# Four small copies inside the chip's memory are issued after the last weight transfer instead of ahead of three

## The chip, the core and the metric

The kernel runs on one core of one Trainium2 chip. A core has a matrix engine (TensorE, "PE" in the profile, with "PEld" for its weight loads), a vector engine (VectorE, "DVE"), a scalar engine (ScalarE, "ACT"), a general engine (GpSimd, "POOL") and a synchronisation engine (SyncE, "SP"). Each has its own instruction stream. Data comes into the on-chip memory (SBUF) and leaves it by 16 DMA engines; POOL, SP and ACT issue such transfers on queues of their own. Matrix products land in PSUM, which has eight banks.

The metric is device time in microseconds (us) of the one core. Lower is better.

## What is computed

Two stages in a row. The first is linear attention with a learned feature map, for 8 batches, 8 heads, 576 rows and 64 channels:

```python
def phi(x):
    proj = einsum('bhsd,df->bhsf', x, w_phi)
    proj = proj - max(abs(proj), axis=-1)
    return concatenate([exp(proj), exp(-proj)], axis=-1)
kv  = einsum('bhsf,bhsd->bhfd', phi(k), v);  z = sum(phi(k), axis=2)
x   = einsum('bhsf,bhfd->bhsd', phi(q), kv) / (einsum('bhsf,bhf->bhs', phi(q), z) + 1e-6)
```

The heads are then laid side by side, so that x is 8 x 576 x 512. The second stage mixes channels in the frequency domain, with one complex 512 x 512 matrix for each of the 64 lowest frequencies:

```python
X = rfft(x, axis=1);  Y = zeros_like(X)
Y[:, :64] = einsum('bmd,mde->bme', X[:, :64], w_r + 1j * w_i)
u = x + irfft(Y, n=576, axis=1)
out = u + relu(u @ w_ch)
```

The weights w_r and w_i are 64 x 512 x 512 each in float32; they are nearly all of the kernel's input.

## The kernel before, in words

**Attention.** Sixteen units (four groups of two heads by four pairs of batches) are worked through in a software pipeline. Their result stays in SBUF as xs, in bf16, and the forward transform of each group is a product with a table of cosines and sines.

**Weights.** The 64 frequencies are handled as eight "octets" o = 0 to 7 of eight frequencies, for each of the four groups g of 128 input channels, and for the real (i = 0) and imaginary (i = 1) matrix. That makes 64 weight tiles of 1 MB in bf16. `wload` (line 341) issues each as one transfer on POOL's queue, which converts from float32 on the way. `next_w` (line 362) takes the next key from the list wq and issues it. A tile pool of nine buffers (tag "wt") holds the tiles. In the last stage four of the buffers are taken by other tiles, so five weights fit. The last 16 keys, those of octets 6 and 7, are the late ones (`LATE`, line 356). A weight is used by `mix` (line 474): eight matmuls into one PSUM tile.

**Last stage.** The loop at line 941 takes the remaining mixes one by one. After each mix it asks for one more weight, with four exceptions (line 954), and then hands out a share of other work: `fill` (line 829) pops steps of a hand-written list with costs in microseconds. The list holds products of x with w_ch (`Channels`, 696), steps that turn finished octets for the inverse transform (`relay`, 795), and steps that add the inverse transform of octets 0 to 5 to all rows (`Absorb`, 736). In `keep_w` (760) half of the Absorb steps have ACT copy a bank to a tile rl, and POOL add it to the tile xw; the rest have ACT write xw itself.

When the last mix of an octet is done, its result y (8 frequencies, real and imaginary, 8 batches: 128 rows of 512) is copied from PSUM to a tile yst. For octets 6 and 7, z = y @ w_ch is also computed and copied to zst. The tiles yst and zst have two buffers each. The "late rows" tile yl holds y and z of octets 6 and 7 turned so that frequency lies on partitions and batch inside: `put` (line 837) moves a 128 x 512 tile to 16 partitions of yl by a transfer from SBUF to SBUF, and each tile goes to two places. For octet 6 POOL issues these four transfers, for octet 7 SP does:

```python
def put(src, o, copies):
    for s in copies:
        r = 32 * s + 16 * (o - 6)
        (pool if o == 6 else sp).dma_start(yl[r:r + 16], src)
```

**Last rows.** The `Last` objects (line 843) finish the output. For each pair of rows `base` brings the two sums (x plus what was absorbed, and its product with w_ch) into PSUM; `late` (876) adds the inverse transform of octets 6 and 7 by matmuls that read yl; the first rows read yst and zst directly instead (`straight`). Then come the relu, the sum and the store, which SP issues. Some of the `base` steps stand ahead of the last mix.

Every engine executes its instructions in the order in which the program makes them (lines are reported as that of a helper, L38, so that groups are told by their tiles). A transfer that POOL or SP issues stands in that engine's stream like any other instruction: what it has to wait for, everything behind it waits for too. Transfers on POOL's queue are taken up in the order of their issue. Eight semaphores are used in turn for them, and a transfer waits until the one that used its semaphore before has landed.

Of the kernel before, what the change touches and what calls it, by code (L numbers as in the profile page):

```python
# [44 lines left out]
def kernel(  # L45
# [295 lines left out]
    def wload(g, w):  # L341
        wt = home(g, w)
        o, i = w // 2, w % 2
        w = (moe_w_r, moe_w_i)[i]
        pool.dma_start(
            wt.rearrange("p m r e -> p m (r e)"),
            w[MG * o:MG * o + MG, g * 128:(g + 1) * 128, :].rearrange(
                "m (p r) e -> p m (r e)", r=2))
        return wt
# [3 lines left out]
    wq = [(g, mg) for g in range(NG) for mg in range(during[g])]  # L353
# [8 lines left out]
    def next_w(n):  # L362
        for _ in range(n):
            if wq:
                key = wq.pop(0)
                wts[key] = wload(*key)
# [107 lines left out]
    def mix(g, w, wt, XT, bank):  # L474

        o, i = w // 2, w % 2
        together = range({6: 2, 7: 0}.get(o, g), NG) if 2 * o >= during[g] else (g,)
        first, last = i == 0 and g == together[0], i == 1 and g == together[-1]
        XT = kept[:, g] if o == 7 and g < 2 else XT[..., 4 * o:4 * o + 4]
        if first:  # L480
            pys[o] = bank()
        py = pys[o]
        for r in range(2):
            for j in range(4):
                pe.matmul(
                    py[32 * j:32 * j + 32, :],
                    lhsT=XT[:, i, r, :, :, :, j].rearrange("p t x b -> p (t x b)"),
                    rhs=wt[:, j, r, :], start=(first and r == 0), stop=(last and r == 1),
                )
        if last and g == 0:  # L490
            act.copy(yacc[:, o, :], pys.pop(o))
        elif last and g < NG - 1:
            dve.tensor_tensor(
                out=yacc[:, o, :], in0=pys.pop(o), in1=yacc[:, o, :], op=ALU.add)
# [103 lines left out]
    def bank(shape=(128, DMODEL), dt=F32):  # L598
        return pst.tile(list(shape), dt, name="pt", tag="pt")
# [195 lines left out]
    def relay(b):  # L795

        assert turned >= (7 if b < 2 else 6)
        at = slice(0, 6 + (b < 2))
        n = 16 * at.stop
        cols = [yTa[:, dc, b, at].rearrange("p o k -> p (o k)") for dc in range(4)]  # L800
        py, pz = two_banks()
        py = py.bitcast(BF16)[:, 0:512]
        for dc in range(4):
            pe.transpose(py[:n, 128 * dc:128 * dc + 128], cols[dc], ident_b)
        for dc in range(4):
            pe.matmul(pz[:n], lhsT=cols[dc], rhs=wchb[:, dc, :],
                      start=(dc == 0), stop=(dc == 3))
        dve.tensor_copy(yall[:n, b], py[:n])
        act.copy(zall[:n, b], pz[:n])
# [14 lines left out]
    for at, b in ((24, 1), (22, 0), (17, 3), (14, 2), (7, 5), (5, 4)):  # L824
        tail.insert(at, (1.25, lambda b=b: relay(b)))
    todo[-2:] = [(1.25, lambda: relay(6)), todo[-2], (1.25, lambda: relay(7)), todo[-1]] + tail
    owed, turned = 0.0, 0

    def fill(n):
        nonlocal owed  # L830
        owed += n
        while todo and owed > 0:
            cost, f = todo.pop(0)
            owed -= cost
# [6 lines that stand above are left out]
# [100 lines left out]
    while mixq:  # L941
        key = mixq.pop(0)
        g, o, i = key[0], key[1] // 2, key[1] % 2
        if key not in wts:
            next_w(1)
        if not mixq:
            assert not todo
            for c in seq[:2]:
                c.base(1)
            for c in (seq[0], seq[2]):  # L950
                c.base(0)
        mix(*key, wts.pop(key), XTb[g % 2], bank)
        left = len(mixq)
        if left not in (LATE + 11, LATE + 1, LATE, LATE - 3):
            next_w(1)
        n = 3.4 if left > 1 else 99.0 if left else 0.0
        if g == NG - 1 and i == 1:
            end = left == 0
            py = pys.pop(o)
            yst = pb.tile([128, DMODEL], BF16, name="yst")  # L960
            pt = [bank([128, 2, 128], BF16) for h in range(2)]
            yT = [pb.tile([128, 2, 128], BF16, name=f"yT{h}") if o > 5 else None
                  for h in range(2)]
            for h in range(2):
                at = slice(H * h, H * h + H)
                if not end:
                    dve.tensor_tensor(out=yst[:, at], in0=py[:, at], in1=yacc[:, o, at],
                                      op=ALU.add)
                elif h:
                    act.copy(yst[:, at], py[:, at])  # L970
                else:
                    dve.tensor_copy(yst[:, at], py[:, at])
            if o > 5:
                put(yst, o, (0, 2))
            if not end:
                fill(0.8 if o != 5 else 0.0)
            for h in range(2):
                for dc in range(2):
                    pe.transpose(pt[h][:, dc, :],
                                 yst[:, H * h + 128 * dc:H * h + 128 * dc + 128], ident_b)  # L980
                src = pt[h].rearrange("p c (k b) -> p c b k", b=B_)
                into = yTa[:, 2 * h:2 * h + 2, :, o] if o < 6 else None
                if h != end:
                    dve.tensor_copy(*((into, src) if o < 6 else (yT[h], pt[h])))
                else:
                    act.copy(*((into, src) if o < 6 else (yT[h], pt[h])))
            turned = o + 1
            if o < 6:
                fill(n - 1.1)
                continue  # L990
            if o == 6:
                for h in range(2):
                    dve.tensor_copy(
                        yTa[:, 2 * h:2 * h + 2, 0:2, 6],
                        yT[h].rearrange("p c (k b) -> p c b k", b=B_)[:, :, 0:2])
            if end:
                seq[0].straight(0)
                seq[0].keep_p()
                seq[2].straight(0, (0,))
            else:  # L1000
                fill(0.8)
            cut = (slice(0, 384), slice(384, DMODEL))
            pz = [bank([128, e.stop - e.start]) for e in cut]
            for e in range(2):
                for h in range(2):
                    for dc in range(2):
                        pe.matmul(
                            pz[e], lhsT=yT[h][:, dc, :], rhs=wchb[:, 2 * h + dc, cut[e]],
                            start=(h == dc == 0), stop=(h == dc == 1))
            zst = pb.tile([128, DMODEL], BF16, name="zst")  # L1010
            act.copy(zst[:, cut[0]], pz[0])
            dve.tensor_copy(zst[:, cut[1]], pz[1])
            put(zst, o, (1, 3))
            fill(n - 2.4 if left else 0)
        else:
            fill(n)
# [70 lines left out]
```

## Time and profile before

| what | value |
|---|---|
| median of 3 runs | 437.31 us (435.58 to 438.34) |
| the profiled execution's own time | 435.97 us |
| its span, first to last instruction | 434.2 us |
| busy: PE / DVE / ACT / POOL | 77% / 69% / 65% / 26% of the span |
| mean granted clock of PE | 0.905 |
| POOL's queue (q0) | 85.27 MB, 100.8% of 16 engines' span |
| weight transfers: size, median time from issue to landing | 1024 KB, 25.4 us (w_r), 25.7 us (w_i) |
| the copies to yl that POOL issues: size, median to landing | 128 KB; 20.9 us (y), 19.5 us (z) |
| the copies to yl that SP issues | 128 KB; 3.6 us (y), 3.8 us (z) |
| stores of pairs of rows | 16 of 512 KB, 3.2 us to landing |

Times inside the execution are microseconds from the start of the span. "Busy" is the time in which an engine had an instruction in work. The granted clock is the share of full speed that the chip let PE run at. A chain of waits is followed back from the last instruction: at each step to what released it, or to the instruction before it on its engine. In the timeline an instruction's wait stands in brackets with what ended it. The name yl<-yst x2 means two transfers that read yst and write yl.

### The profile page before, as it was taken

What the parts mean: (1) busy time and instruction counts of PE and PEld (TensorE: products, weight loads), DVE (VectorE), ACT (ScalarE), POOL (GpSimd) and SP (SyncE); (2) the same over time, 40 slices, a digit from 0 to 9 for tenths busy, and PEclk for the clock granted to TensorE, in tenths of its full rate; (3) what the DMA queues carried; (4) which work ended last, traced back from release to release, by engine and by line L of the source; (5) the groups of instructions that cost most, each with busy time, mean ns of one, the idle gap of its engine ahead of it and who ended that gap; (6) DMA issues with size and microseconds to landing.
All of it is one profiled execution on the core that took longest, in us unless ns stands there. A gap on an engine that the chain in (4) does not pass through costs nothing.

```text
span 434.2 us, 10105 instructions
## 1 busy us (share of the span) xinstructions
PE 336.4 (77%) x4208; PEld 202.1 (47%) x4252; DVE 298.6 (69%) x585; ACT 283.2 (65%) x483; POOL 114.4 (26%) x154
## 2 busy tenths in 40 slices
PE   2577778688688578786787787957899999968994
PEld 1345556555465455554554555633344444423321
DVE  5668686765886866977977878696634447643685
ACT  3787696786986966877876877435344456643782
POOL 6232132123221412322221210210121047530073
PEclk9979697789998976989998988988899999997998
DMA  9999999999999999999999999999999999996788
GB/s 214 209 212 209 238 212 237 232 218 239 237 211 239 213 234 264 211 239 212 235 227 216 246 226 210 211 212 212 212 212 212 212 211 212 217 201 114 242 346 332
DMA packets 49821, 97.71 MB, mean 225 GB/s; under 512 B 2288, under 2 KB 11632, under 8 KB 49776
## 3 DMA queue, kind: packets, MB, share of 16 engines
q0 software_dynamic: 45088, 85.27, 100.8%
q1 hardware_dynamic: 4528, 11.73, 7.4%
q8 instruction: 33, 0.54, 0.4%
q10 hardware_dynamic: 160, 0.07, 0.1%
q14 instruction: 12, 0.10, 0.1%
HBM read 163.64 MB, written 9.44 MB: 399 GB/s over the span
## 4 chain that ended last, share of the span: by engine, by line
PE 42%; DVE 22%; ACT 16%; DMA 12%; issue 6%; POOL 0%; POOLq 0%; ACTq 0%; DVEq 0%
PE pt L38 15%; PE one L38 15%; PE two L38 8%; ACT AB L38 7%; DMA wt<-in_moe_w_i_dram 5%; DVE mk L38 5%; DVE m L38 5%; DMA kb<-in_k_dram 5%; PE pp L38 4%; ACT AQ L38 3%; ACT XT L38 2%; DVE xs L38 2%; DMA qb<-in_q_dram 2%; DVE XT L38 2%; DVE yacc L38 1%
## 5 line engine op out<-in xcount | busy, mean ns | idle before, releaser
L38 ACT ACTIVATE AB<-two 128x1024 bf16<-128x1024 f32 x64 | 62.0, 1024 | 11.0 <-DVE mk L38 8.3
L38 ACT ACTIVATE AQ<-two 128x1024 bf16<-128x1024 f32 x64 | 62.6, 1045 | 2.1 <-PE two L38 2.0
L38 DVE TENSOR_REDUCE m<-two 128x8 f32<-128x1024 f32 x32 | 39.2, 1224 | 17.2 <-PE two L38 17.1
L38 ACT CAST xw<-pt 128x512 bf16<-128x512 f32 x45 | 26.4, 586 | 36.6 <-PE pt L38 36.6
L38 PE MATMUL pt<-wchb,xT 128*128 128x512 bf16 x135 | 38.9, 400 | 9.3 <-DVE xT L38 7.3
L38 POOL DMA_DIRECT2D wt<-in_moe_w_r_dram x30 | 22.4, 747 | 87.6 <-PE pt L38 39.9
L38 DVE TENSOR_REDUCE mk<-two 128x8 f32<-128x1024 f32 x32 | 38.9, 1217 | 7.7 <-PE two L38 7.7
L38 DVE TENSOR_TENSOR va<-vn,ee 128x1152 bf16<-128x1152 f32 x32 | 42.2, 1361 | 0.0
L38 PE MATMUL two<-w2blk,qT 128*128 128x256 bf16 x128 | 23.5, 315 | 21.4 <-ACT AB L38 9.8
L38 POOL DMA_DIRECT2D wt<-in_moe_w_i_dram x28 | 21.0, 750 | 65.4 <-PE one L38 36.8
L38 PEld LDWEIGHTS <-xs 128*128 128x128 bf16 x624 | 31.5, 102 | 12.5 <-issue 6.0
L38 ACT COPY qT<-one 128x512 bf16<-128x512 bf16 (+1 forms) x32 | 19.4, 641 | 25.6 <-PE one L38 25.2
L38 PEld LDWEIGHTS <-qT 128*128 128x128 bf16 x144 | 15.1, 107 | 36.0 <-issue 31.7
L38 PE MATMUL two<-mT,minus 96*128 96x512 bf16 x64 | 27.0, 423 | 3.1 <-issue 1.1
L38 PEld LDWEIGHTS <-AQ 128*128 128x128 bf16 x512 | 24.2, 107 | 7.9 <-issue 4.3
L38 DVE TENSOR_TENSOR xs<-one,rd 128x384 bf16<-128x384 f32 x48 | 26.7, 557 | 1.6
L38 PE MATMUL two<-w2blk,kT 128*128 128x256 bf16 x128 | 20.6, 288 | 9.2 <-ACT AB L38 9.2
L38 PE MATMUL one<-kvz,AQ 128*128 128x65 bf16 x512 | 26.9, 207 | 1.0 <-ACT qT L38 0.8
L38 DVE COPY xT<-pt 128x512 bf16<-128x512 bf16 x36 | 16.8, 470 | 14.9 <-PE pt L38 14.9
L38 DVE RECIPROCAL rd<-one 128x6 f32<-128x6 f32 x48 | 9.4, 195 | 25.2 <-PE one L38 25.2
L38 PE MATMUL one<-wt,XT 128*32 128x512 bf16 x272 | 24.7, 452 | 1.7 <-DMA kb<-in_k_dram 1.7
L38 PEld LDWEIGHTS <-xT 128*128 128x128 bf16 x168 | 15.3, 103 | 21.9 <-DVE xT L38 8.0
(163 smaller groups left out, 735.8 us busy)
## 6 DMA issues: line engine op xcount, KB each, us to landing
wt<-in_moe_w_r_dram POOLq DMA_DIRECT2D x30, 1024.0 KB, 25.4
wt<-in_moe_w_i_dram POOLq DMA_DIRECT2D x28, 1024.0 KB, 25.7
out_dram<-of SPq DMA_DIRECT2D x16, 512.0 KB, 3.2
vn<-in_v_dram POOLq DMA_DIRECT2D x13, 576.0 KB, 23.6
kb<-in_k_dram POOLq DMA_DIRECT2D x16, 288.0 KB, 19.2
qb<-in_q_dram POOLq DMA_DIRECT2D x16, 288.0 KB, 17.0
xs<-in_moe_w_i_dram POOLq DMA_DIRECT2D x2, 1024.0 KB, 23.8
vn<-in_v_dram SPq DMA_DIRECT2D x3, 576.0 KB, 5.3
```

What stands on the lines that cost most here:

```text
L38: ins = f(*args, **kwargs)
```

## The change

The tile pair of octet 6 is kept in a variable `staged` instead of being copied at once. In the loop, after each possible issue of a weight, the four copies are issued if the list of weights is empty and the pair has not been copied yet. For octet 7 (`end` is true) the copies stay where they were, on SP.

```diff
-    owed, turned = 0.0, 0
+    owed, turned, staged = 0.0, 0, None
...
         left = len(mixq)
         if left not in (LATE + 11, LATE + 1, LATE, LATE - 3):
             next_w(1)
+        if not wq and staged:
+            put(staged[0], 6, (0, 2))
+            put(staged[1], 6, (1, 3))
+            staged = None
         n = 3.4 if left > 1 else 99.0 if left else 0.0
...
-            if o > 5:
+            if end:
                 put(yst, o, (0, 2))
             if not end:
                 fill(0.8 if o != 5 else 0.0)
...
             dve.tensor_copy(zst[:, cut[1]], pz[1])
-            put(zst, o, (1, 3))
+            if end:
+                put(zst, o, (1, 3))
+            else:
+                staged = yst, zst
             fill(n - 2.4 if left else 0)
```

In the changed program the order of instructions is the same on PE, DVE, ACT and SP. On POOL the four copies move from between the fourth- and third-last weight transfers to just after the last one. Three weight transfers and five of POOL's additions (xw<-rl,xw) that stood behind the first copies, or between them, now stand ahead of them.

## The prediction

> **What bounds the kernel now.** I read the page's slices and queues first, then the chain of work that ended last, then POOL's and PE's order of time around the change, and last the clock by windows.
>
> From the page: busy share of the DMA engines and GB/s in 40 slices of 10.85 us, and the share of POOL's transfer queue.
>
> ```profile
> DMA  9999999999999999999999999999999999996788
> GB/s 214 209 212 209 238 212 237 232 218 239 237 211 239 213 234 264 211 239 212 235 227 216 246 226 210 211 212 212 212 212 212 212 211 212 217 201 114 242 346 332
> q0 software_dynamic: 45088, 85.27, 100.8%
> ```
>
> The engines are full until slice 36, at about 212 GB/s in the second half: the kernel waits for its weights, which all go through q0, POOL's queue. The chain (start, us, what) says how that ends:
>
> ```profile
> 375.98 0.83 PE pp L38 x3
> 377.26 22.25 DMA wt<-in_moe_w_i_dram
> 401.86 1.30 PE pt L38 x10
> ```
>
> The last weight is asked for at 377.26 and lands at 399.51; after it come about 35 us of last rows, mostly PE, DVE and stores, in which PE stands at 1.00 busy from 402 to 426. So the time is the landing of the last weight plus that tail. POOL around the change (start, us, instruction, what it waited for):
>
> ```profile
> 361.53 0.78 POOL L38 DMA_DIRECT2D wt<-in_moe_w_r_dram  x1
> 362.31 1.09 POOL L38 DMA_DIRECT2D yl<-yst  x2
> ...
> 365.43 1.05 POOL L38 DMA_DIRECT2D yl<-zst  x2
> ...
> 367.59 0.79 POOL L38 DMA_DIRECT2D wt<-in_moe_w_i_dram  x1
> ...
> 372.34 0.79 POOL L38 DMA_DIRECT2D wt<-in_moe_w_r_dram  x1 [2.77 <-DMA wt<-in_moe_w_r_dram]
> ...
> 377.26 0.78 POOL L38 DMA_DIRECT2D wt<-in_moe_w_i_dram  x1 [1.85 <-PE pp L38]
> ```
>
> The four copies stand in q0 ahead of the last three weights. **What they cost the queue** follows from times to landing, asked for one issue at a time: 20.3, 22.1, 22.2 and 22.25 us for these four weights, so they land at 381.8, 389.7, 394.5 and 399.5. Two weights with nothing between them are 4.9 us apart, the two with the copies between them 7.8 to 7.9. The four copies (0.5 MB) hold q0 for **2.9 us**.
>
> PE at the end (start, us, instruction, wait):
>
> ```profile
> 389.68 1.08 PE L38 MATMUL pt<-wt,XT 128*32 128x512 bf16 x8 [3.71 <-DMA wt<-in_moe_w_i_dram]
> ...
> 396.86 0.66 PE L38 MATMUL pt<-wt,XT 128*32 128x512 bf16 x8
> ...
> 399.55 0.66 PE L38 MATMUL pt<-wt,XT 128*32 128x512 bf16 x8 [0.63 <-DMA wt<-in_moe_w_i_dram]
> 400.74 0.69 PE L38 MATMUL pt<-ident_b,yst 128*128 128x128 bf16 x4 [0.53 <-DVE yst L38]
> ```
>
> PE ran dry at 385.8, stood 3.7 us for one weight, had its remaining filler work at 391 to 396.5, and stood 0.6 us for the last weight. And the clock (window, its length, busy us of PE, PEld, DVE, ACT, POOL, granted clock, DMA):
>
> ```profile
> 197.77:201.18 3.41, 1.70 (x18) 1.30 (x21) 2.33 (x4) 2.55 (x5) 0.00 (x0) 1.00 1.16 209
> ...
> 286.52:289.93 3.41, 1.63 (x19) 0.85 (x18) 3.04 (x23) 1.07 (x2) 0.74 (x1) 1.00 1.12 214
> 289.93:293.34 3.41, 2.70 (x12) 1.25 (x10) 3.27 (x7) 1.67 (x3) 0.00 (x0) 0.50 1.12 211
> ...
> 385.50:388.92 3.42, 0.47 (x3) 0.13 (x1) 1.14 (x2) 1.43 (x3) 0.18 (x1) 1.00 1.12 213
> 388.92:392.33 3.41, 2.65 (x12) 0.78 (x12) 0.14 (x1) 0.00 (x0) 0.00 (x0) 0.50 1.12 212
> 392.33:395.74 3.41, 3.41 (x9) 1.06 (x7) 1.84 (x3) 1.73 (x3) 0.00 (x0) 0.50 0.92 174
> ```
>
> The granted clock changes in this trace only at steps of a grid of 3.41 us. A window in which PE was busy 1.63 us is followed by half clock, one with 1.70 is not: below about half busy, the next window is halved. A halved window gives the clock back only if it was nearly full: after 2.65 and 2.70 it stayed halved, after 3.41 it came back. So the 3.7 us wait cost 6.8 us of half clock, which today lies on filler work and ends just before the last weight lands.
>
> **The change part by part.**
>
> *Copies behind the last weight.* No instruction is added or removed. On POOL four issues of 0.53 to 0.56 us move past three weight issues and five additions. q0 carries the same bytes, so its last weight lands 2.9 us earlier, at 396.6, and the copies end where the queue ends today, about 399.5. The first row that reads them is a matmul at 408.6 today, 405.7 then: 6 us to spare. They now meet SP's four copies of the eighth octet (issued at 401.1 to 403.7, so from 398.2 on) for some 1.3 us. The last of those lands at about 407.5 against the read at 408.6, a cover of 1.1 us; gone, it would cost 0.2 us. I take nothing.
>
> *POOL's waits.* In the changed order the copies wait for the landings of two earlier weights (issued 349.45 and 352.32, landed 22.3 and 24.4 us later: 371.8 and 376.7) that the last two weight issues wait for today. The last copy is thus issued near 377.3, and the addition behind it starts near 377.8, against 378.06 today: no cost. The weight issues lose those waits; they come one to three us earlier into a queue 20 us deep, which moves no landing. If the addition were held for one weight more (4.9 us), the ACT copies and banks of the filler work would follow; PE has about 2.9 us of standing time then, so up to 2 us would show. Two tiles kept: both have two buffers and the eighth octet takes the other one, so no wait.
>
> *PE, up to the last weight.* The third-last mix starts at 389.7 − 2.9 = 386.8 after an idle of 1.0 us instead of 3.7; its window is then about 2.4 us busy, so no half clock. Today 389.68 to 396.86 is 7.2 us, 6.1 of them halved; at full clock 4.2 us. PE is through at 391.0 and waits for the next weight until 391.6 (394.5 − 2.9); the mix and the base matmuls (396.86 to 398.92 today, 2.1 us) end at 393.7. The last weight lands at 396.6, so **PE stands 2.9 us** right ahead of the tail.
>
> *PE, in the tail.* On this profile's grid PE is busy 1.4 us of 392.33:395.74, under half: the clock is halved at 395.74, and the next window (0.9 us standing, 0.5 us waiting for DVE's copy) is not full, so it stays halved until 402.57. The path then pays: the mix 1.0 for 0.6 us (as at 389.68), +0.4; four transposes about +0.2; and from 399.3 to 402.57 half of 3.3 us, +1.65, as PE is the tail's bound there. Together **2.3 us**. Bounds: nothing if no window falls under half; 3.4 (two whole windows in the tail) above. On other positions of the grid, the same steps lose 0.9 to 2.9 us; 2.3 is this profile's own.
>
> **Sum** against the profiled execution (435.97, span 434.2): − 2.9 + 2.3 = −0.6, **435.4**. That execution was quick: the median of the runs is 437.31 (435.58 to 438.34), 1.3 above it. Part of that spread I put down to the grid: where the half clock of the 3.7 us wait comes late or short, PE stands longer before the last weight and loses again after it. So against the median the gain is larger, about 1.9 us or 0.4%, under the 1% that a measurement of this kernel can tell from no change.
>
> [...]
>
> **Rivals.**
>
> *A. The clock holds*: the gap falls across two windows that both stay over half busy, or the tail has slack to take it up. For: 1.70 us was enough once. Against: 2.9 us of idle and 0.5 more leave few positions of the grid. 435.97 − 2.9 = **433.1**, about 1% under the median.
>
> *B. The landing does not move*: the last weight is late because of the slowest of the 16 engines, which the copies do not delay as much; DMA share falls from 0.92 to 0.30 over 394 to 399, so some are done 5 us before others. Against: 7.8 against 4.9 us between landings that count the slowest engine too. 435.97 + 0, **436.0**.
>
> *C. Slower: the half clock costs more than the copies did.* Place: the first 6.8 us after 396.6. Price: two whole windows, 3.4 us, against 2.9 won: +0.5, **436.5** on the profile's own time, 437.8 where the run stands as the median does to the profile. It decides from the point where more than 5.8 us of halved clock lie on PE work behind the last weight, that is where the standing PE loses its clock at 396.6 or after.
>
> *D. It doesn't do what it says*: POOL is held by the copies and the filler slides as above, up to 2 us: about **437.4**.
>
> **Chances.** Forecast 0.58, A 0.14, B 0.10, C 0.12, D 0.06. Range: A's 433.1 and the 437.8 of C, which D lies in; 433.0 to 437.8. Faster by over 1% needs 432.9, the better half of A: 0.07. Slower by over 1% needs 441.7, which only C or D with a cost twice theirs reaches: 0.06. Within 1%: 0.87.
>
> **What would show it.** Last weight's landing at 396.6 and the copies' near 399.5; PE's waits for weights about 1.0, 0.6 and 2.9 us; clock 1.00 around 387 to 391 and 0.50 behind the last mix; no wait for yl. Wrong if PE's wait before the last mix is short, or if the tail from the last mix to the end is not some 2 us longer than today's.

## The result, and the profile after

The changed kernel takes 435.15 us (median of 20 runs, 433.55 to 436.38), the kernel before 437.48 us beside it (20 runs, 435.54 to 438.90). The ratio is 0.9945, with a 95% interval of 0.9930 to 0.9961. The forecast was 435.4. The profiled execution took 434.07 us, its span is 432.3.

POOL in order of time in the changed kernel (start, us, instruction, idle time before it and what ended it):

```profile
367.54 0.78 POOL L38 DMA_DIRECT2D wt<-in_moe_w_r_dram  x1
...
371.87 0.78 POOL L38 DMA_DIRECT2D wt<-in_moe_w_i_dram  x1
372.64 1.09 POOL L38 DMA_DIRECT2D yl<-yst  x2
373.72 0.53 POOL L38 DMA_DIRECT2D yl<-zst  x1
376.65 0.53 POOL L38 DMA_DIRECT2D yl<-zst  x1 [2.40 <-DMA wt<-in_moe_w_i_dram]
377.20 3.38 POOL L38 TENSOR_TENSOR xw<-rl,xw 128x512 bf16<-128x512 f32 x3
```

The copies now stand behind the last weight. The last of them waits for an earlier weight to land, and the additions behind it start at 377.20, where they started at 378.06 before.

The chain that ended last (start, us, what) still ends its transfer part with the last weight:

```profile
371.87 24.36 DMA wt<-in_moe_w_i_dram
396.27 0.69 PE pt L38 x8
```

It lands at 396.23 instead of 399.51. To see how much of that is the copies, take a weight well ahead of them in both traces: the one asked for at 328.5 before landed 28.4 us later, at 356.9; the same weight was asked for at 326.7 after and took 29.8, so 356.5. In the view of the transfers (size, us from issue to landing), first before, then after:

```profile
wt<-in_moe_w_i_dram POOLq DMA_DIRECT2D x1, 1024.0 KB, 28.4
...
wt<-in_moe_w_i_dram POOLq DMA_DIRECT2D x1, 1024.0 KB, 29.8
```

From there to the last landing it was 42.6 us and is 39.7: **2.9 us**, the predicted size; the other 0.4 us arose earlier in the execution. The gap of 7.9 us between two landings, where the copies stood, is gone: the last four weights now land at 381.4, 386.8, 391.2 and 396.2, none more than 5.4 us after the one ahead of it.

PE in order of time in the changed kernel:

```profile
386.89 0.66 PE L38 MATMUL pt<-wt,XT 128*32 128x512 bf16 x8 [1.39 <-DMA wt<-in_moe_w_i_dram]
...
391.45 0.66 PE L38 MATMUL pt<-wt,XT 128*32 128x512 bf16 x8
...
396.27 0.66 PE L38 MATMUL pt<-wt,XT 128*32 128x512 bf16 x8 [2.75 <-DMA wt<-in_moe_w_i_dram]
397.46 0.80 PE L38 MATMUL pt<-ident_b,yst 128*128 128x128 bf16 x4 [0.53 <-DVE yst L38]
398.48 0.63 PE L38 MATMUL pp<-yst,CF 128*128 128x512 bf16 x1 [0.22 <-issue]
398.90 1.91 PE L38 MATMUL pt<-wchb,yT 128*128 128x384 bf16 x8
```

The 3.7 us wait is 1.4 us, the next weight is waited for no more than before, and the wait for the last one has grown from 0.6 to 2.75 us. Right behind it the matmuls are slow: a single one of 512 columns is 0.63 us, and the eight whose product becomes zst take 1.91 us. In the kernel before, the same two groups were:

```profile
401.48 0.38 PE L38 MATMUL pp<-yst,CF 128*128 128x512 bf16 x1
401.70 1.04 PE L38 MATMUL pt<-wchb,yT 128*128 128x384 bf16 x8
```

The clock in windows of its grid in the changed kernel (window, length, busy us of PE, PEld, DVE, ACT, POOL, granted clock, DMA):

```profile
390.62:394.03 3.41, 2.84 (x18) 0.96 (x17) 1.33 (x2) 1.35 (x3) 0.00 (x0) 1.00 1.01 211
394.03:397.44 3.41, 0.66 (x8) 0.20 (x7) 0.42 (x1) 0.01 (x1) 0.00 (x0) 1.00 0.54 127
397.44:400.86 3.42, 3.17 (x14) 1.81 (x16) 0.29 (x2) 1.75 (x4) 0.00 (x0) 0.50 0.33 79
400.86:404.27 3.41, 3.41 (x17) 1.41 (x16) 1.96 (x4) 2.13 (x6) 0.00 (x0) 1.00 0.46 100
```

In 394.03:397.44 PE was busy 0.66 us; the next window is halved, and it lies on the tail. From the start of the last mix to the end of the span it was 434.2 − 399.55 = 34.65 us and is 432.3 − 396.27 = 36.03: **1.4 us of the 2.9 are given back** in this execution. A second profile of the changed kernel (its repeat below) shows the same: a wait of 3.07 us, a halved window from 396.57 to 399.98, and 431.8 − 395.92 = 35.9 us from the last mix to the end.

### The profile page after: what moved, and what is told of

Same layout as the page of the kernel before. It is cut to its first block, busy times and chain, and to the rows that moved or that the text cites. A ratio compares the mean times of both kernels' runs of the same rounds, so it can differ in the third digit from the quotient of the medians.

```text
span 432.3 us, 10106 instructions
## 1 busy us (share of the span) xinstructions
PE 329.0 (76%) x4208; PEld 199.9 (46%) x4252; DVE 298.2 (69%) x585; ACT 283.0 (65%) x483; POOL 115.2 (27%) x154
## 4 chain that ended last, share of the span: by engine, by line
PE 34%; DMA 19%; issue 15%; DVE 14%; ACT 13%; POOL 3%; POOLq 0%; ACTq 0%; DVEq 0%
PE pt L38 15%; PE one L38 9%; DMA wt<-in_moe_w_r_dram 7%; DMA wt<-in_moe_w_i_dram 6%; PE two L38 5%; DMA kb<-in_k_dram 5%; ACT AB L38 5%; DVE m L38 4%; PE pp L38 4%; ACT AQ L38 3%; DVE mk L38 3%; DMA qb<-in_q_dram 2%; POOL wt L38 2%; ACT XT L38 2%; ACT xw L38 1%
## 5 line engine op out<-in xcount | busy, mean ns | idle before, releaser
L38 PE MATMUL pt<-wchb,xT 128*128 128x512 bf16 x135 | 37.1, 385 | 10.3 <-DVE xT L38 8.2
L38 PE MATMUL two<-w2blk,qT 128*128 128x256 bf16 x128 | 20.9, 289 | 21.9 <-ACT AB L38 10.2
L38 PEld LDWEIGHTS <-qT 128*128 128x128 bf16 x144 | 14.2, 101 | 36.4 <-issue 33.3
L38 PE MATMUL two<-mT,minus 96*128 96x512 bf16 x64 | 28.2, 440 | 3.6 <-issue 1.8
L38 POOL DMA_DIRECT2D kb<-in_k_dram x16 | 11.4, 714 | 54.8 <-PE one L38 46.5
```

The lines of the kernel that those rows point to most:

```text
L38: ins = f(*args, **kwargs)
```

## The experiments

Each is compared with the kernel before on its own chip, whose median there stands beside it. The added matmuls of several experiments read constant tiles and write a PSUM bank that nobody reads.

**The clock in the tail, after the change.** Ten added matmuls ahead of the last mix fill the time in which PE stands:

```diff
+    def spin(n):
+        t = bank()
+        for _ in range(n):
+            pe.matmul(t, lhsT=ident_b, rhs=wchb[:, 0, :], start=True, stop=True)
...
             for c in (seq[0], seq[2]):
                 c.base(0)
+            spin(10)
```

> The changed kernel, with ten matmuls of 128x512 whose result nobody reads, right ahead of the last mix (10 x 0.216 = 2.2 us of the 2.75 us that PE stands there). My theory (the standing costs half clock in the tail): no window falls under half busy, the clock stays at 1.00 from 390 to 425, the tail from the last weight's landing to the end is back at about 34.7 us, and the time is 433.3 to 433.9, 1.2 to 1.8 below the changed kernel's 435.15, with less spread between runs. Rival (the tail is longer for another reason, such as the copies meeting SP's): 435.1, unchanged. Second rival (added matmuls are late for the last mix): slower than 435.15.

Measured: 432.41 us against 436.60, ratio 0.9910 (0.9889 to 0.9932), six runs within 0.30 us of each other. The kernel before is 0.9 us quicker on this chip (436.60) than in the first comparison (437.48); by the ratios (0.9910 and 0.9945) the matmuls win 1.5 us, as expected. PE in order of time:

```profile
392.50 2.32 PE L38 MATMUL pt<-wchb,ident_b 128*128 128x512 bf16 x10
396.02 0.67 PE L38 MATMUL pt<-wt,XT 128*32 128x512 bf16 x8 [1.20 <-DMA wt<-in_moe_w_i_dram]
397.21 0.69 PE L38 MATMUL pt<-ident_b,yst 128*128 128x128 bf16 x4 [0.53 <-DVE yst L38]
...
398.17 1.04 PE L38 MATMUL pt<-wchb,yT 128*128 128x384 bf16 x8
```

The eight matmuls that took 1.91 us take 1.04, and the tail is 430.7 − 396.02 = 34.7 us again. So in the profiled execution the tail was longer because of the clock and nothing else.

Both kernels were run once more, on one chip:

> The changed kernel itself, beside the next one on the same chip: ratio 0.9935 to 0.9955, spread of runs over 2 us.

> The changed kernel with ten unread matmuls ahead of the last mix, again, beside the changed kernel on the same chip: 1.2 to 1.8 us below it, spread of runs under 0.8 us. If the first result was a chip's or a chance's, the two are level.

The changed kernel 434.56 us (433.54 to 435.12; ratio 0.9947, 0.9927 to 0.9967), with the matmuls 432.34 us (432.20 to 432.53; ratio 0.9902, 0.9876 to 0.9929), the kernel before 436.74. The difference is 2.2 us, more than the 1.4 of the one profiled execution and more than was expected here; the sign and the narrow spread hold. The changed kernel's own runs spread over 1.6 us, not the 2 expected. Both of its profiled executions were among the quicker ones (434.07 and 433.54), so what the longer ones lose is known from their times alone. This version beats both kernels.

**The clock in the kernel before.** The kernel before gets 14 such matmuls ahead of the third-last mix and ten ahead of the last one:

```diff
+            spin(10)
...
+        if len(mixq) == 2:
+            spin(14)
         mix(*key, wts.pop(key), XTb[g % 2], bank)
```

> The kernel before, with 14 such matmuls (3.0 us) in the 3.7 us wait ahead of the third-last mix and ten (2.2 us) ahead of the last. My theory: half clock vanishes from 386 on; what is left against the changed kernel with its ten matmuls is the place of the copies in the queue alone, 2.6 to 3.0 us. Time 436.2 to 436.8, about 1 below the kernel before (437.48), whose median has some half clock in the tail too. Rival (half clock in the kernel before is always hidden in the wait for the last weight): 437.5, as before.

Measured: 435.23 us against 436.60, ratio 0.9979 (0.9962 to 0.9997). That is 1.4 us won without touching a transfer: the kernel before, too, lost something to its clock in most executions, and more than the 1 us expected. Six of its 23 runs on this chip took 434.9 to 435.1 us without help; ten of the twelve with the matmuls took 434.9 to 435.6. The clean price of the copies' place is the difference to the first experiment: 435.23 − 432.41 = **2.8 us**, and the profiles agree, with the last mix at 398.81 here against 396.02 there:

```profile
398.81 0.66 PE L38 MATMUL pt<-wt,XT 128*32 128x512 bf16 x8 [0.95 <-DMA wt<-in_moe_w_i_dram]
```

Then the 14 matmuls alone, without the ten:

> The kernel before, with the 14 matmuls in the 3.7 us wait ahead of the third-last mix only. PE is then at full clock for its filler, is done with it some 2.5 us sooner and stands 2.9 us for the last weight, as in the changed kernel. My theory: the half clock moves from the filler into the tail, and the 1.4 us that both sets of matmuls won are lost: ratio 0.999 to 1.003, about as before, against 0.9979 with both sets. If half clock anywhere costs and its removal helps anywhere: 0.997 to 0.998.

Measured: 437.28 us against 436.53, ratio 1.0017 (1.0000 to 1.0035). Its PE line of the last mix:

```profile
398.54 1.08 PE L38 MATMUL pt<-wt,XT 128*32 128x512 bf16 x8 [3.15 <-DMA wt<-in_moe_w_i_dram]
```

and its clock:

```profile
394.39:397.80 3.41, 0.99 (x5) 0.39 (x4) 0.00 (x0) 0.17 (x1) 0.00 (x0) 1.00 0.59 112
397.80:401.22 3.42, 2.15 (x14) 0.73 (x14) 0.72 (x2) 0.61 (x2) 0.00 (x0) 0.50 0.01 2
```

The filler runs at full clock (0.38 us for one of its matmuls, 0.63 in the kernel before) and is done early, PE stands 3.15 us, and the half clock has moved into the tail, which takes 435.5 − 398.54 = 37.0 us, against 34.65 in the kernel before. The faster stage ahead of the transfer that ends last gained nothing here, and cost what comes behind.

**How short a gap must be.** The changed kernel with four matmuls instead of ten:

> The changed kernel with four such matmuls (0.9 us) ahead of the last mix instead of ten: PE then stands some 2.0 us for the last weight and 0.5 us behind the mix, never near a whole window of 3.4 us. By half a window of work as the threshold (the rows of the kernel before), the clock still falls in some positions of the grid and not in others: two groups of runs, lowest as with ten matmuls (0.991 of the kernel before), median 0.992 to 0.995. If only a gap of about a whole window costs the clock, none falls and all runs are as with ten matmuls: 0.990 to 0.992 with a spread under 0.7 us.

Measured: 432.70 us against 436.53, ratio 0.9921 (0.9892 to 0.9950), six runs: 432.19, 432.30, 432.36, 433.04, 433.71 and 435.33. Most are as good as with ten, one takes as long as the longest of the changed kernel's second set (435.12). The profiled run kept its clock although PE stood for long:

```profile
395.75 0.66 PE L38 MATMUL pt<-wt,XT 128*32 128x512 bf16 x8 [2.37 <-DMA wt<-in_moe_w_i_dram]
```

The runs spread over 3.1 us, so the second reading (only a gap of about a whole window costs) fails. The grid stood elsewhere in each execution: a window began at 391.86 here, at 394.03 and 393.16 in the two profiles of the changed kernel. That its place decides whether the same gap costs the clock is the author's estimate from these places and the spread of the times: none of this version's longer runs was profiled, and six runs are few to give the shares.

"Under half busy" is a rough line, too. In the trace of the kernel before it does part the windows from 17 us on: behind every one at full clock with PE busy 1.68 us or less (160.22:163.63 is the one with 1.68) the clock is halved, behind those with 1.70 us or more it is not. Here the wait fell across two windows, 391.86:395.27 with PE busy 1.52 us and 395.27:398.69 with 2.29 us, and the clock stayed at 1.00. In the trace of the changed kernel, windows with 1.26 us (281.39:284.80) and 1.64 us (288.21:291.62) kept the clock as well, and one with 1.75 us (131.20:134.61) lost it. "Nearly full" is no firmer: in that trace the clock came back after a halved window with 2.71 us (134.61:138.02) and stayed halved after one with 2.82 us (182.40:185.81).

**The copies left out.** Where the changed kernel issues the copies, POOL fills yl with zeros instead (3.5 us on POOL), so y and z of the seventh octet are missing from the late rows:

```diff
-            put(staged[0], 6, (0, 2))
-            put(staged[1], 6, (1, 3))
+            pool.memset(yl, 0.0)
```

> The changed kernel without the four copies: y and z of the seventh octet are left out of the late rows, which hold zeros there instead (POOL fills the tile where it issued the copies). If copies behind the last weight cost nothing, as the prediction has it, the time is the changed kernel's, 434.7 to 435.6. If they disturb the last weight's transfer or SP's copies of the eighth octet, it is 0.5 to 1.5 below, 433.7 to 434.6.

Measured: 434.43 us against 436.60, ratio 0.9951 (0.9932 to 0.9969). In microseconds alone that would lie in the second range, but this is the chip on which the kernel before is 0.9 us quicker, and the ratio is the changed kernel's (0.9945 and 0.9947). The profile agrees: from the landing of the weight used as the mark above to the last landing it is 39.7 us, as with the copies, and from the last mix to the end 432.0 − 396.12 = 35.9 us. Behind the last weight the copies cost nothing that these runs can tell.

**Half of the change.** Only the copies of z are late:

> Half of the change: the two copies of y stay in their old place, the two of z go behind the last weight. Bytes on the engines set the price: the gap between the landings around the y copies is 6.3 to 6.5 us instead of 7.8 or 4.9, the last weight lands 1.4 us earlier than before, PE stands about 2 us ahead of the last mix, which sometimes costs the clock and sometimes not. Ratio 0.9955 to 0.998, between the two kernels, with a wide spread of runs (over 2 us). Were the price one of position (any copy ahead of the weights), the landing would not move and the ratio be 1.00.

Measured: 435.07 us against 436.53, ratio 0.9972 (0.9954 to 0.9990), between the two kernels. The weight asked for at 328.8 landed 27.2 us later, at 356.0, and the last one at 397.2: 41.2 us, where the kernels have 42.6 and 39.7. Half the bytes, half the time. The runs spread over 2.0 us (434.29 to 436.30); PE stood 3.34 us ahead of the last mix in the profile, not the 2 us expected, since the filler now ran at full clock as well (0.38 us for one of its matmuls).

**Another queue.** The kernel before, with the four copies issued by SP in the same place of the program:

```diff
-            (pool if o == 6 else sp).dma_start(yl[r:r + 16], src)
+            sp.dma_start(yl[r:r + 16], src)
```

> The kernel before, with the seventh octet's four copies issued by SP in the same place of the program, so they stand in no queue ahead of a weight and POOL never waits for them. If the copies cost the transfer engines' time wherever they are issued ahead of the last weight, the last weight lands as in the kernel before and the time is the same: ratio 0.997 to 1.003. If the cost comes from POOL's queue or from POOL's waits, the weights go by 2.9 us earlier and the ratio is that of the changed kernel, about 0.9945 or lower.

Measured: 436.83 us against 436.53, ratio 1.0002 (0.9986 to 1.0019). That looks like a plain "bytes cost the same anywhere", but the profile says otherwise. The weight asked for at 328.4 landed at 356.7 and the last at 398.3, 41.6 us later: one us sooner than in the kernel before. PE's line shows where it went:

```profile
398.36 0.67 PE L38 MATMUL pt<-wt,XT 128*32 128x512 bf16 x8 [3.10 <-DMA wt<-in_moe_w_i_dram]
```

In the window 396.40:399.81 PE was busy 0.92 us, the next one (399.81:403.22) is halved (0.63 us for a single matmul of 512 columns), and from the last mix to the end it is 434.7 − 398.36 = 36.3 us instead of 34.65.

The matmuls ahead of the last mix were added to this kernel to take the clock out:

> The kernel before with the four copies issued by SP in their old place, and ten unread matmuls ahead of the last mix, so that the clock no longer hides the landing. In the profile of the run without the matmuls the last weight landed 41.6 us after the weight that POOL asked for at about 328 us, against 42.6 in the kernel before and 39.7 in the changed one: the copies then cost 1.9 us on SP's queue, not 2.9. If that is so and the half clock took back the rest, the ratio is now 0.9950 to 0.9960. If SP's copies cost the full 2.9 us: 0.9975 to 0.9985. If nothing: 0.991.

Measured: 434.57 us against 436.74, ratio 0.9965 (0.9947 to 0.9984). Beside the changed kernel with the same matmuls on the same chip (432.34) that is 2.2 us; by the profiles, last mix at 397.44 against 395.91 of the other, 1.5 us. The two lines, first SP's copies, then the changed kernel, both with the ten matmuls:

```profile
397.44 0.66 PE L38 MATMUL pt<-wt,XT 128*32 128x512 bf16 x8 [0.96 <-DMA wt<-in_moe_w_i_dram]
...
395.91 0.66 PE L38 MATMUL pt<-wt,XT 128*32 128x512 bf16 x8 [1.20 <-DMA wt<-in_moe_w_i_dram]
```

So the copies on SP's queue cost more than nothing, 1.5 to 2.2 us. That this is less than on POOL's queue does not follow from the times (the intervals of 0.9965 here and of 0.9979 above overlap), but from the landings: from the mark to the last weight it is 42.5 to 42.7 us in the three profiles with POOL's copies ahead of the last weights, 41.4 and 41.6 in the two with SP's, and 39.7 to 39.9 in the six with the copies behind or left out. More than half of the price stays when the copies leave POOL's queue; the author puts that part down to the bytes on the engines, which is an estimate from these landings. Why it is smaller on SP's queue stays open.

**The copies twice, which told something else.** The kernel before, with each copy of the seventh octet issued two times:

```diff
-            (pool if o == 6 else sp).dma_start(yl[r:r + 16], src)
+            for _ in range(2 if o == 6 else 1):
+                (pool if o == 6 else sp).dma_start(yl[r:r + 16], src)
```

> The kernel before, with each of POOL's four copies issued twice in its old place (the same bytes to the same rows). If the copies cost the queue's time, the gap between the landings around them grows from 7.8 to 10.6 us and the time by 2.6 to 3.2 us: 440.1 to 440.7. If the cost was POOL's waiting in its order (weight issues late) or the slowest engine has slack, less than 1.5 us more.

Measured: 454.68 us against 436.60, ratio 1.0419 (1.0392 to 1.0445): 18 us, not 3. POOL in order of time:

```profile
366.90 0.56 POOL L38 DMA_DIRECT2D yl<-yst  x1
381.90 1.06 POOL L38 DMA_DIRECT2D yl<-yst  x2 [14.45 <-DMA yl<-yst]
386.25 0.53 POOL L38 DMA_DIRECT2D yl<-yst  x1 [3.28 <-DMA yl<-yst]
...
397.32 0.79 POOL L38 DMA_DIRECT2D wt<-in_moe_w_i_dram  x1
```

The second copy writes the rows of the first and so waits 14.45 us until the first has landed, behind a queue of weights; everything behind it on POOL waits as well, and the next weight is asked for only at 397.32, when no other weight is left in the queue: the last one was asked for at 366.12, ahead of the copy that had landed by 381.90. The forecast of 3 us failed, and the run says nothing of the price of the bytes. It shows what a wait of POOL for a transfer of its own queue costs.

## Why the prediction was right

**The queue.** "The four copies hold q0 for 2.9 us": 2.9 us between landings in the changed kernel, 2.8 us between the two kernels without clock losses, half of it for half of the copies. Rival B (the landing does not move) has fallen.

**Copies behind the last weight cost nothing.** Confirmed by leaving them out. They land up to 398.6 (asked for at 376.65 and 21.9 us), and the first matmul that reads yl starts at 406.7 without a wait.

**POOL's waits.** The wait of 2.40 us is the one foreseen, and the additions start 0.9 us earlier than before, so rival D has fallen. In the kernel before, the row of the last weight's issue names PE; that the issue waited for a landing, as the prediction read it, fits the changed kernel, where the same issue waits for nothing and the last copy waits for that landing (350.57 and 25.8 us, so 376.4; the transfer is the eighth ahead of it on POOL's queue). "One to three us earlier" was 2.0, 4.8 and 5.4 us for the three weight issues (the last from 377.26 to 371.87), but 1.8 us of each this execution had won before, at the issue ahead of them (361.53 to 359.78). These weights still took over 21 us from issue to landing, and nothing points to a landing that this moved.

**PE up to the last weight.** Waits of 1.0, 0.6 and 2.9 us were forecast, 1.39, none shown, and 2.75 measured; the clock stayed at 1.00 from 384 to 397. (PE ran dry at 385.97 in the kernel before, not at 385.8, so the first wait came out of the prediction's own rows as 0.8.)

**The tail.** A halved window came behind the wait, as forecast, but its cost was not the forecast's in this execution: +2.3 us were taken, from two halved windows on the grid of the profile before; the grid stood elsewhere, one window was halved (397.44 to 400.86), and the tail grew by 1.4. The prediction had 0.9 to 2.9 for other positions of the grid. Over many runs the loss was 1.5 us by the ratios of the first pair and 2.2 by the medians of the second (434.56 − 432.34), so the 2.3 is at the upper end.

**The sum.** 435.97 − 2.9 + 2.3 = 435.4 was made against one execution, and the profiled execution after is at 435.97 − 3.3 + 1.4 = 434.07. So on the profile for which it was made the forecast was 1.3 us too high. Against the medians it was 1.9 us won, measured 2.3. That 435.4 comes within 0.3 us of the median, 435.15, is partly luck: the sum took off 0.6 us, where the two profiles differ by 1.9, and it started from a quick run of the kernel before, 1.5 us under the median of its 20 runs. The runs give the parts, taken on different chips: 2.8 us of queue, plus 1.4 that the kernel before loses to its own clock, minus 2.2 that the changed one loses, 2.0 us. That the kernel before loses anything was the guess on its spread, and it held: with both sets of matmuls it wins 1.4 us (by the ratio's interval 0.1 to 1.7), and its runs spread over 1.6 us instead of 3.3. With PE kept at work the changed kernel's runs lie within 0.3 us, where they spread over 2.8 without. Why a few runs of the kernel before with both sets of matmuls stay high (12 runs, 434.91 to 436.54) stays open.

**Rivals A and C.** The clock did not hold at a gap of 2.75 us with 0.53 us of waiting behind it (PE busy 0.66 us in its window, the next one halved), so A has fallen for this kernel; with four matmuls (0.9 us) more, and a wait of 2.4 us, the time was near the best in most of six runs, so A was not far away. C (the half clock costs more than the copies) did not come: 1.4 against 2.9 us in the profiles, 2.2 against 2.8 by the medians.

## What to carry to other kernels

Where one queue is full until the last input lands, what can wait belongs behind that input: here 0.5 MB of copies inside the chip, needed only 10 us after it had landed, held the last weight by 2.8 us. Then look at what stands idle because the input is still the last to come: the wait that became longer halved PE's clock on the stage that sets the end and took back 1.4 us of the gain in the profile, up to 2.2 by the medians, and a few useless matmuls in the wait brought it back. When a kernel's runs spread by 3 us without a cause, look at such gaps.

## What the runs showed that was not expected

The four copies cost 2.8 us on POOL's queue and only 1.5 to 2.2 us on SP's, beside the same weights; the landings show the difference, its cause stays open. And a test on the time alone would have read that experiment wrongly (ratio 1.0002), because what the earlier landing won was taken back by the clock.
